# Order of the expert weights' loads around the last writes of x in a three-stage kernel

## The chip, the cores and the metric

The kernel runs on one core of one Trainium2 chip. A core has five engines with queues of their own: PE (TensorE, matmuls into PSUM), DVE (VectorE), ACT (ScalarE), POOL (GpSimd) and SP (SyncE, which here issues the loads and stores). They wait for each other through semaphores. Sixteen DMA engines move data between DRAM and SBUF. The metric is the device time of one execution in microseconds (us).

## What is computed

The reference chains three stages for 2 batches of 768 tokens, all in float32. First a linear attention with 8 heads of 64 and a decaying state. Then a feed-forward block with a gate, 512 to 1024 to 512 columns, whose hidden values pass through a convolution over three tokens. Then a mixture of 8 experts, of which each token uses one:

```
def _attn_ref(q, k, v):
    for t in range(S):
        state = gamma * state + einsum('bhd,bhe->bhde', k[:, :, t], v[:, :, t])
        y[:, :, t] = scale * einsum('bhd,bhde->bhe', q[:, :, t], state)

def _moe_ref(x, w_in, conv_w, w_out):
    h = maximum(x @ w_in, 0)
    conv_out = sum of conv_w[k] * (h moved by k - 1 tokens), k = 0, 1, 2
    return (h * sigmoid(conv_out)) @ w_out

def _moe2_ref(x, w_gate, w_local, w1, w2):
    logits = x @ w_gate;  local = sigmoid(x @ w_local)
    for each token s:  e = argmax(logits[s]) if s == 0 or local[s] < 0.5 else the e before it
        out[s] = softmax(logits[s])[e] * (maximum(x[s] @ w1[e], 0) @ w2[e])
```

## The kernel before, in words

The order of all instructions is written out by hand; the program runs straight on, and nothing reorders it on the chip except that each engine waits for what its next instruction needs.

The second stage's output for one group of 128 tokens is `x_ps` in PSUM (`ffn_out`). ACT copies it to SBUF (`xn`, for the last two groups `xl`, L501), and SP writes it to the DRAM buffer `xs` (L503). Each batch has six groups. In the second batch, four of the six writes are from `xn` and the fifth and sixth from `xl`. The units of this last part are counted by `n`, one for each group and block of 128 hidden columns; the fourth group is complete at `n` = 24, the fifth at 32, the sixth at 40.

The third stage works on tiles of 128 tokens that share an expert. GpSimd gathers a tile's tokens from `xs` by an index table `it` (`gather`, L740 and L741: a memset of the tile `xg`, then an indirect DMA of 256 KB). The first two gathers (tiles 0 and 1, issued at `n` = 27) read only the rows of the first ten writes; the tokens of the last two groups reach tiles 0 and 1 from `xl` in SBUF by four matmuls with one-hot matrices (`late_x`, L836). The third gather is that of the first quarter tile, and it and all later ones read all of `xs`, so they wait for the sixth write.

A tile is turned with matmuls against the identity (L830 for tiles 0 and 1, L817 else), multiplied by w1 (`g1`, PSUM tile `g`), put through a relu by ACT (`hr`, L868), turned again, and multiplied by w2 (`g2`, PSUM tile `y`). There is one PSUM tile `g`, so a tile's first product starts when ACT has read the one before. The result goes out scaled (`yo`, L879) by a scatter of GpSimd (L880). For accuracy each product is three matmuls of a high and a low part (`mm3`, L133 to L135); ACT and DVE make the two parts of the weights (`cut`, L731 and L732) into slots `ws0h`, `ws0l`, `ws1h` and `wc`.

Weights come by SP. `fetch(j, which)` issues four loads of 512 KB of tile j's w1 or w2 into the raw buffer `r` (L710). From tile 2 on a load carries a condition and moves nothing if the tile two before it had the same expert. `fetch_q(g, which, i)` loads four pieces of 512 KB for a quarter tile (L722): tokens of four experts, 32 of each, share one tile. The pieces alternate between two buffers, `qc` and `qs1l`. A group of quarters (`group`) is a generator: one step turns the gathered quarters and ACT copies them to `xq` (L901), the next ones multiply (`hq_ps`, L909, then `yq_ps`, L931). `QT` lists the numbers of the calls of `hook()` at which the next step is emitted; tiles 0 and 1 have the first two calls, and every later tile four.

All of SP's transfers are in one queue in the order of the program. Their landings are told by eight semaphores taken in turn, so SP issues a transfer when the one eight before it has landed.

Of the kernel before, what the change touches and what calls it, by code (L numbers as in the profile page):

```python
# [91 lines left out]
def tile_kernel(ctx, tc, cat, cst, qT, kT, kN, vN, w_in, conv_w, w_out, wg, w1, w2, out):  # L92
# [393 lines left out]
    def ffn_out(b, t, ms):  # L486

        ts = slice(t * P, (t + 1) * P)
        if ms[0] == 0:
            OUT[b, t] = psb.tile([P, DM], F32, tag="x2", name="x2_ps")  # L490
        ps = OUT[b, t]
        for m in ms:
            g = hg[b, m]
            mm3(ps, g[:, 0, ts], g[:, 1, ts], wo_hi[:, m, :], wo_lo[:, m, :], m == 0, m == 7)
        if ms[-1] == 7:
            if b == B - 1 and t >= NG - 2:
                xn = xpool[0].tile([P, DM], F32, name=f"xl{t}", bufs=1)
                LAST.append(xn)
            else:
                xn = rt.tile([P, DM], F32, name="xn", bufs=2)  # L500
            se.activation(out=xn, in_=OUT.pop((b, t)), func=AF.Copy)  # L501
            r = b * S + t * P
            sy.dma_start(out=xs[r:r + P, :], in_=xn)  # L503
# [183 lines left out]
    def home(tag):  # L687
        return big if tag[0] == "s" else ws if tag == "c4" else wx

    def expert_at(n):  # L690
        return sy.value_load(ei[0:1, 0, n:n + 1], min_val=0, max_val=E - 1)

    def raw(lane, which):
        if (lane, which) not in RAW:
            RAW[lane, which] = (wx if lane and which else ws).tile([P, 4, 1024], F32, name=f"r{lane}{which}")
        return RAW[lane, which]

    def fetch(j, which, parts=range(4)):

        src = (w1, w2)[which].rearrange("e p a n -> e p (a n)")  # L700
        kw = {}
        if j == 0:
            src = src[0]
        else:
            src = src[bass.ds(expert_at(j), 1)].rearrange("o p n -> (o p) n")
            if j > 1:
                kw = dict(cond=sy.value_load(ei[0:1, 1, j:j + 1], min_val=0, max_val=1), cond_hint=True)
        dst = raw(j % 2, which)
        for i in parts:
            sy.dma_start(out=dst[:, i, :], in_=src[:, i * 1024:(i + 1) * 1024], **kw)  # L710

    def fetch_q(g, which, i, parts=range(4)):

        if (g, which, i) not in QW:
            tag = QSLOT[nq[0] % 2]
            nq[0] += 1
            QW[g, which, i] = home(tag).tile([P, 4, 1024], F32, tag=tag, name="q" + tag)
        w = QW[g, which, i]
        src = (w1, w2)[which].rearrange("e p a n -> e p (a n)")
        for u in parts:  # L720
            one_e = src[bass.ds(expert_at(NTILE + 4 * g + u), 1)].rearrange("o p n -> (o p) n")
            sy.dma_start(out=w[:, u, :], in_=one_e[:, i * 1024:(i + 1) * 1024])  # L722

    def cut(j, which, i):

        tag = SLOT[ncut[0] % len(SLOT)]
        ncut[0] += 1
        w = home(tag).tile([P, 2, 2, 1024], F32R, tag=tag, name="w" + tag)
        for h in range(2):
            r = RAW[j % 2, which][:, 2 * i + h, :]  # L730
            se.activation(out=w[:, 0, h, :], in_=r, func=AF.Copy)  # L731
            ve.tensor_tensor(out=w[:, 1, h, :], in0=r, in1=w[:, 0, h, :].bitcast(F32), op=ALU.subtract)  # L732
        W[j, which, i] = w.rearrange("p s h n -> p s (h n)")
# [3 lines left out]
    def gather(j, n=NT):  # L737

        X[j] = xg = xpool[0].tile([P, DM], F32, name="xg")
        po.memset(xg, 0.0)  # L740
        return po.indirect_dma_start(out=xg, out_offset=None, in_=xs[0:n], in_offset=bass.IndirectOffsetOnAxis(ap=it[:, j:j + 1], axis=0),  # L741
                                     bounds_check=n - 1, oob_is_err=False)
# [45 lines left out]
    for n, (t, m) in enumerate(units, 1):  # L788
        ffn_out(1, t, (m,))
        for step in STEPS.get(n, ()):  # L790
            next(step, done)
        if n in (18, 24):
            fetch(1, 0, range(2) if n == 18 else range(2, 4))
        if n in (20, 28):
            cut(0, 0, n // 28)
        if n == 27:
            for j in range(2):
                gather(j, NT - 2 * P)
        if n in (27, 32):
            fetch_q(0, 0, 0, range(3) if n == 27 else range(3, 4))  # L800
    p2_stack.close()
    q_stack.close()
    lg_stack.close()
# [133 lines left out]
                yield  # L937


    QT = [3, 8, 8, 9, 13, 18] + [19, 22, 26, 26, 27, 31, 36]  # L940
    groups = []
    hooks = [0]

    def hook():
        hooks[0] += 1
        while QT and QT[0] <= hooks[0]:
            QT.pop(0)
            while groups and next(groups[0], done) is done:
                groups.pop(0)

    def experts(n):

        fetch(1, 1)
        fetch_q(0, 0, 1)
        for j in range(2):
            begin_x(j)
        for j in range(2):
            turn_x(j)
        gather(NTILE)
        gather(2)  # L960
        groups.extend(group(g, g + 1 < QSTAT) for g in range(QSTAT))
        h = tile_g1()
        for i in range(2):
            g1(0, i, h)
            cut(1, 0, i)
            if i:
                relu(0, h)
            hook()
        cut(0, 1, 0)
        fetch(2, 0)  # L970
        T = {}
        for j in range(n):
            last, ahead = j + 1 == n, j + 2 < n
            if j + 3 < n:
                fetch(j + 3, 0)
            if j > 0:
                finish(j - 1)
            if j + 3 < n:
                gather(j + 3)
            if j == 2:  # L980
                gather(NTILE + 1)
            if j not in T and j > 0:
                T[j] = turn_h(j)
            if not last:
                h = tile_g1()
                g1(j + 1, 0, h)
                if j == 0:
                    next(groups[0])
                    T[j] = turn_h(j)
                    cut(0, 1, 1)  # L990
                if ahead:
                    cut(j + 2, 0, 0)
                hook()
                g1(j + 1, 1, h)
                if ahead:
                    cut(j + 2, 0, 1)
                relu(j + 1, h)
                hook()
            if ahead:
                turn_x(j + 2)  # L1000
                fetch(j + 2, 1)
            Y[j] = y = psb.tile([P, 512], F32, tag="b", name="y")
            for i in range(2):
                g2(j, i, T[j], y)
                if not last:
                    cut(j + 1, 1, i)
                    if not ahead and i == 0:
                        T[j + 1] = turn_h(j + 1)
                    hook()
        finish(n - 1)  # L1010
        assert not QT

# [68 lines left out]
```

## Time and profile before

| | us |
|---|---|
| median of 3 runs | 427.65 (425.49 to 429.69) |
| the profiled execution | 422.35 |
| its span, first to last instruction | 420.5 |
| PE busy | 402.5 (96%) |
| DVE busy | 290.1 (69%) |
| ACT busy | 256.3 (61%) |
| POOL busy | 93.7 (22%) |

The page is taken from one execution. Busy times are sums over the span, and a stage can be full on an engine whose share of the whole is low. A row of a timeline has its start, its length, the engine, the line and the tile written and read (out<-in); what the engine waited for stands in brackets. For SP a row is the issue of transfers, not the transfers. In the row of a stretch, the DMA share is the mean busy share of the sixteen DMA engines, and it can come out a little above 1, since a packet counts with its whole length where it starts.

### The profile page before, as it was taken

How to read it: one execution, taken by the hardware profiler on the slowest of the kernel's cores; microseconds unless marked ns; L12 is line 12 of the kernel's file. 1: busy time of each engine (PE TensorE's matmuls, PEld its weight loads, DVE VectorE, ACT ScalarE, POOL GpSimd, SP SyncE). 2: the span in 40 equal slices, each digit the busy share in tenths (PEclk: the TensorE clock that was granted, in tenths of full speed). 3: DMA queues.
4: the chain of work that ended last, by engine and by line, in shares of the span. 5: the costliest groups of instructions: out<-in, count | busy, mean ns of one | idle time of the engine just before them, and what ended most of it. 6: DMA issues, size and time to landing. Idle time of an engine off the chain costs nothing.

```text
span 420.5 us, 7242 instructions
## 1 busy us (share of the span) xinstructions
PE 402.5 (96%) x2412; PEld 328.2 (78%) x2412; DVE 290.1 (69%) x494; ACT 256.3 (61%) x405; POOL 93.7 (22%) x92
## 2 busy tenths in 40 slices
PE   8999999999999999999999789999998999999991
PEld 7898999998987888988778676776766667676881
DVE  3789989798873630578997077959673885958650
ACT  2787778578663323666514178868574786858560
POOL 4356756230200000000001220305304202201210
PEclk9999999999999999999999999999999999999997
DMA  7989872330000101000398999999969999684100
GB/s 238 391 298 397 283 243 60 102 85 16 2 2 0 64 38 50 2 0 2 112 339 311 391 365 345 338 408 409 399 251 367 371 377 388 242 257 197 45 23 33
DMA packets 27324, 86.59 MB, mean 206 GB/s; under 512 B 3598, under 2 KB 4622, under 8 KB 27280
## 3 DMA queue, kind: packets, MB, share of 16 engines
q1 hardware_dynamic: 25200, 79.76, 51.7%
q0 software_dynamic: 2080, 6.29, 3.8%
q8 instruction: 21, 0.34, 0.3%
q14 instruction: 23, 0.19, 0.1%
HBM read 105.18 MB, written 6.55 MB: 266 GB/s over the span
## 4 chain that ended last, share of the span: by engine, by line
PE 47%; issue 25%; DMA 18%; DVE 4%; POOL 2%; ACT 1%; SPq 1%; POOLq 0%
DMA out_dram<-yo,it 16%; PE h_ps L133 6%; PE x_ps L133 6%; PE h_ps L134 5%; PE h_ps L135 5%; PE x_ps L135 5%; PE x_ps L134 5%; PE y L303 3%; PE s_ps L283 3%; PE y L305 2%; PE lg L356 2%; PE wc_ps L194 2%; DMA kq<-in_qT_dram 1%; DMA xs<-xl 1%; POOL xg L741 1%
## 5 line engine op out<-in xcount | busy, mean ns | idle before, releaser
L880 POOL DMA_INDIRECT out_dram<-yo,it x13 | 17.0, 1311 | 133.1 <-ACT yo L879 133.1
L133 PE MATMUL h_ps<-xT,wih 128*128 128x384 f32 x128 | 46.6, 364 | 0.1
L741 POOL DMA_INDIRECT xg<-xs,it x13 | 18.9, 1451 | 121.4 <-DMA r<-in_w_dram 111.1
L365 DVE SCALAR_TENSOR_TENSOR cc<-h,cw,cc 128x768 f32<-128x768 f32 x32 | 34.8, 1088 | 15.8 <-ACT cc L362 15.8
L134 PE MATMUL h_ps<-xT,wih 128*128 128x384 f32 x128 | 43.1, 337 | 0.0
L135 PE MATMUL h_ps<-xT,wil 128*128 128x384 f32 x128 | 43.0, 336 | 0.0
L133 PE MATMUL x_ps<-woh,hg 128*128 128x512 f32 x96 | 38.5, 401 | 0.0
L135 PE MATMUL x_ps<-woh,hg 128*128 128x512 f32 x96 | 37.5, 391 | 0.0
L134 PE MATMUL x_ps<-wol,hg 128*128 128x512 f32 x96 | 37.5, 390 | 0.0
L154 POOL TENSOR_TENSOR na<-na,raw 128x512 int32<-128x512 int32 (+1 forms) x17 | 23.0, 1354 | 50.8 <-DVE na L152 25.8
L732 DVE TENSOR_TENSOR ws0h<-r,ws0h 128x1024 fp32r<-128x1024 f32 x22 | 26.0, 1222 | 8.0 <-ACT ws0h L731 8.0
L732 DVE TENSOR_TENSOR ws1h<-r,ws1h 128x1024 fp32r<-128x1024 f32 x22 | 26.0, 1222 | 8.0 <-ACT ws1h L731 6.0
L732 DVE TENSOR_TENSOR wc<-r,wc 128x1024 fp32r<-128x1024 f32 x22 | 26.0, 1221 | 7.9 <-ACT wc L731 7.9
L303 PE MATMUL y<-at,vz 128*128 128x128 f32 x192 | 29.5, 275 | 0.8 <-ACT vz L278 0.8
L732 DVE TENSOR_TENSOR ws0l<-r,ws0l 128x1024 fp32r<-128x1024 f32 x22 | 26.0, 1221 | 6.2 <-ACT ws0l L731 6.0
L283 PE MATMUL s_ps<-qz,kq 128*128 128x256 f32 x96 | 29.1, 386 | 1.0 <-DVE qz L252 1.0
L731 ACT ACTIVATE wc<-r 128x1024 fp32r<-128x1024 f32 x22 | 22.1, 1055 | 11.2 <-PE g L135 11.2
L731 ACT ACTIVATE ws0l<-r 128x1024 fp32r<-128x1024 f32 x22 | 22.1, 1057 | 9.0 <-PE y L135 9.0
L303 PEld LDWEIGHTS y<-at,vz 128*128 128x128 f32 x192 | 25.9, 192 | 1.4 <-ACT vz L278 1.0
L133 PEld LDWEIGHTS h_ps<-xT,wih 128*128 128x128 f32 x128 | 24.1, 189 | 3.3 <-issue 2.1
L285 DVE TENSOR_TENSOR at<-s_ps,ca 128x256 f32<-128x256 f32 x48 | 20.2, 420 | 8.2 <-PE s_ps L283 7.6
L501 ACT ACTIVATE xn<-x_ps 128x512 f32<-128x512 f32 x10 | 6.0, 597 | 31.1 <-PE x_ps L135 13.8
(234 smaller groups left out, 1036.0 us busy)
## 6 DMA issues: line engine op xcount, KB each, us to landing
r<-in_w_dram SPq DMA_DIRECT2D x88, 512.0 KB
qc<-in_w_dram SPq DMA_DIRECT2D x32, 512.0 KB
qs1l<-in_w_dram SPq DMA_DIRECT2D x32, 512.0 KB
raw<-in_w_in_dram SPq DMA_DIRECT2D x8, 512.0 KB
raw<-in_w_out_dram SPq DMA_DIRECT2D x8, 512.0 KB
kq<-in_qT_dram SPq DMA_DIRECT2D x7, 384.0 KB
kq<-in_kT_dram SPq DMA_DIRECT2D x7, 384.0 KB
kv<-in_vN_dram SPq DMA_DIRECT2D x7, 384.0 KB
```

The source lines that it names most:

```text
L133: te.matmul(ps, lhi, rhi, start=first, stop=False)
L134: te.matmul(ps, lhi, rlo, start=False, stop=False)
L135: te.matmul(ps, llo, rhi, start=False, stop=last)
L154: po.tensor_tensor(out=a, in0=a, in1=lo, op=ALU.add)
L283: te.matmul(ps, self.kq[:, 0, tok], self.qz[:, :, tok], start=True, stop=True)
L285: ve.tensor_tensor(out=self.at[c], in0=ps, in1=self.dm, op=ALU.mult)
L303: te.matmul(y, vz[:, c, j, :], at[:, j, :], start=(j == 0), stop=(c == 0 and j == 1))
L365: ve.scalar_tensor_tensor(out=cc, in0=h[:, i:i + S], scalar=cw[:, m, i:i + 1], in1=cc, op0=ALU.mult, op1=ALU.add)
L731: se.activation(out=w[:, 0, h, :], in_=r, func=AF.Copy)
L732: ve.tensor_tensor(out=w[:, 1, h, :], in0=r, in1=w[:, 0, h, :].bitcast(F32), op=ALU.subtract)
L741: return po.indirect_dma_start(out=xg, out_offset=None, in_=xs[0:n], in_offset=bass.IndirectOffsetOnAxis(ap=it[:, j:j + 1], axis=0), bound ...
L880: po.indirect_dma_start(out=out, out_offset=bass.IndirectOffsetOnAxis(ap=it[:, j:j + 1], axis=0), in_=yo, in_offset=None, bounds_check=NT ...
```

## The change

Three things move, and nothing is added or left out. The loads of tile 1's w1, before in two halves at `n` = 18 and 24, and the first four quarter pieces, before at 27 and 32, are issued behind the fifth write (`n` = 32), except two of the pieces, which come behind the sixth (`n` = 40). The quarters' second piece is issued ahead of tile 1's w2 instead of behind it. And the step that turns the quarters is emitted earlier for the first group (hook 2 instead of inside tile 0's turn) and later for the second group (hook 20 instead of 19).

```
@@ -789,15 +789,15 @@
-        if n in (18, 24):
-            fetch(1, 0, range(2) if n == 18 else range(2, 4))
...
-        if n in (27, 32):
-            fetch_q(0, 0, 0, range(3) if n == 27 else range(3, 4))
+        if n == 32:
+            fetch(1, 0)
+        if n in (32, 40):
+            fetch_q(0, 0, 0, range(2) if n == 32 else range(2, 4))
...
-    QT = [3, 8, 8, 9, 13, 18] + [19, 22, 26, 26, 27, 31, 36]
+    QT = [2, 3, 8, 8, 9, 13, 18] + [20, 22, 26, 26, 27, 31, 36]
...
     def experts(n):
 
+        fetch_q(0, 0, 1)
         fetch(1, 1)
-        fetch_q(0, 0, 1)
...
                 if j == 0:
-                    next(groups[0])
                     T[j] = turn_h(j)
```

SP's queue before, from the second batch's third write of `xn` on. `r_2037` takes tile 1's w1, `qc_2338` the first quarter piece; the rows left out are the reading of the expert's number and what else comes with each issue.

```order
L503 DMA xs<-xn 128x512 x3
...
L710 DMA r_2037<-in_w_dram 128x1024
...
L503 DMA xs<-xn 128x512
...
L710 DMA r_2037<-in_w_dram 128x1024
...
L722 DMA qc_2338<-in_w_dram 128x1024
...
L503 DMA xs<-xl_2389 128x512
...
L722 DMA qc_2338<-in_w_dram 128x1024
L503 DMA xs<-xl_2427 128x512
...
L710 DMA r_2460<-in_w_dram 128x1024
...
L722 DMA qs1l<-in_w_dram 128x1024
```

The same place of the changed kernel; `r_2492` takes tile 1's w2.

```order
L503 DMA xs<-xn 128x512 x4
L503 DMA xs<-xl_2336 128x512
...
L710 DMA r_2037<-in_w_dram 128x1024
...
L722 DMA qc_2352<-in_w_dram 128x1024
...
L503 DMA xs<-xl_2398 128x512
...
L722 DMA qc_2352<-in_w_dram 128x1024
...
L722 DMA qs1l<-in_w_dram 128x1024
...
L710 DMA r_2492<-in_w_dram 128x1024
```

Before, two loads of `r_2037` stand on each side of the fourth write, three pieces ahead of the fifth write and one ahead of the sixth. Now the fourth and fifth writes follow each other, and four loads and two pieces stand between the fifth and the sixth; the other two pieces and the four of `qs1l` are ahead of w2.

PE between tile 0's first product (`g_2550`) and the quarters' product, before:

```order
L135 MATMUL g_2550<-ws0l,xl 128x512
L133 MATMUL g_2642<-ws1h,xh 128x512
...
L135 MATMUL g_2642<-ws1h,xl 128x512
L817 MATMUL tp<-cs,xg 128x128 x4
L817 MATMUL tp<-cs,hr 128x128 x8
L909 MATMUL hq_ps<-qc_2338,xq 32x512 x8
```

And of the changed kernel:

```order
L135 MATMUL g_2541<-ws0l,xl 128x512
L817 MATMUL tp<-cs,xg 128x128 x4
L133 MATMUL g_2640<-ws1h,xh 128x512
...
L135 MATMUL g_2640<-ws1h,xl 128x512
L817 MATMUL tp<-cs,hr 128x128 x8
L909 MATMUL hq_ps<-qc_2352,xq 32x512 x8
```

The four transposes of the gathered quarters (`tp<-cs,xg`) moved from behind the first half of tile 1's first product (12 matmuls) to ahead of it.

ACT at the same place, where the copy of those transposes (`xq`) passes the cut of w2 of tile 0 into `ws0h`; before:

```order
L868 ACTIVATE hr<-g_2550 128x512 x2
L731 ACTIVATE ws0h<-r_2032 128x1024 x2
L901 ACTIVATE xq<-tp 128x512
L821 ACTIVATE th<-tp 128x512 x2
L731 ACTIVATE ws0l<-r_2032 128x1024 x2
```

And of the changed kernel:

```order
L868 ACTIVATE hr<-g_2541 128x512 x2
L901 ACTIVATE xq<-tp 128x512
L731 ACTIVATE ws0h<-r_2032 128x1024 x2
L821 ACTIVATE th<-tp 128x512 x2
L731 ACTIVATE ws0l<-r_2032 128x1024 x2
```

The copy moved one cut up; everything else of ACT is in the same order here.

## Rows read from the trace of the kernel before

**Rows 1.** The page, part 1: engine, busy us (share of the span) and instructions.
```profile
PE 402.5 (96%) x2412; PEld 328.2 (78%) x2412; DVE 290.1 (69%) x494; ACT 256.3 (61%) x405; POOL 93.7 (22%) x92
```

**Rows 2.** Stretches: us, busy us (count) by engine, granted clock, DMA share, GB/s.
```profile
224.00:232.00 8.00, 8.00 (x38) 6.66 (x38) 4.49 (x11) 1.16 (x2) 2.76 (x3) 1.00 1.00 383
248.00:274.00 26.00, 25.56 (x152) 17.69 (x156) 20.93 (x21) 20.97 (x28) 3.75 (x3) 1.00 0.94 341
274.00:310.00 36.00, 36.00 (x199) 27.07 (x192) 25.99 (x26) 26.48 (x36) 9.87 (x8) 1.00 1.02 404
```

**Rows 3.** PE's timeline, 233 to 253 us: start, us, line, instructions [idle before <- releaser].
```profile
235.78 1.13 PE L830 MATMUL tp<-cs,xg 128*128 128x128 f32 x8 [2.22 <-DMA xg<-xs,it]
...
248.44 0.50 PE L133 MATMUL g<-ws1h,xh 128*128 128x512 f32 x1 [1.18 <-ACT hr L868]
...
251.30 0.60 PE L817 MATMUL tp<-cs,xg 128*128 128x128 f32 x4
251.74 1.04 PE L817 MATMUL tp<-cs,hr 128*128 128x128 f32 x8
```

**Rows 4.** SP's timeline, DMA issues: start, us from first to last of a row.
```profile
205.72 3.73 SPq L710 DMA_DIRECT2D r<-in_w_dram  x8
...
221.74 0.91 SPq L710 DMA_DIRECT2D r<-in_w_dram  x2
222.75 0.37 SPq L503 DMA_DIRECT2D xs<-xn  x1
223.92 0.88 SPq L710 DMA_DIRECT2D r<-in_w_dram  x2
225.59 2.61 SPq L722 DMA_DIRECT2D qc<-in_w_dram  x3
228.75 0.33 SPq L503 DMA_DIRECT2D xs<-xl  x1
```

**Rows 5.** GpSimd's timeline, the gathers' starts.
```profile
228.96 1.21 POOL L741 DMA_INDIRECT xg<-xs,it  x1 [111.14 <-DMA r<-in_w_dram]
...
231.00 1.01 POOL L741 DMA_INDIRECT xg<-xs,it  x1 [0.28 <-POOL xg L740]
...
239.77 1.00 POOL L741 DMA_INDIRECT xg<-xs,it  x1 [7.23 <-DMA xs<-xl]
```

**Rows 6.** The chain of waits, 234 us: start, us, what.
```profile
234.22 4.78 DMA xs<-xl
```

**Rows 7.** Tile xg, 225 to 420 us: time from a gather's start to its landing.
```profile
DMA to landing us min/median/max: 4.2/7.0/7.9
```

**Rows 8.** DMA, 205 to 212 us in 40 slices of 0.175 us: rate.
```profile
GB/s 0 0 0 0 0 0 0 0 0 94 70 94 187 234 304 328 257 398 445 398 398 398 468 421 398 374 421 328 398 304 375 445 421 374 375 351 375 468 351 445
```

**Rows 9.** ACT's timeline, two cuts of weights.
```profile
248.28 2.01 ACT L731 ACTIVATE ws0h<-r 128x1024 fp32r<-128x1024 f32 x2
...
262.67 2.01 ACT L731 ACTIVATE ws0h<-r 128x1024 fp32r<-128x1024 f32 x2
```

**Rows 10.** PE's timeline, the gap at 321 us.
```profile
321.84 0.66 PE L817 MATMUL tp<-cs,xg 128*128 128x128 f32 x4 [0.85 <-ACT yo L879]
```

**Rows 11.** SP's timeline and wait at 311.8 us, and PE's timeline behind it.
```profile
311.82 0.07 SPq L710 DMA_DIRECT2D r<-in_w_dram  x1
SPq L710 <- DMA qs1l<-in_w_dram: 0.9, 1, 0.9
312.11 1.90 PE L931 MATMUL yq_ps<-qs1l,tq 128*32 128x512 f32 x16
```

**Rows 12.** Stretches around PE's last matmul, columns as in rows 2.
```profile
410.00:412.00 2.00, 1.92 (x9) 1.26 (x7) 0.00 (x0) 0.00 (x0) 0.00 (x0) 1.00 0.07 25
415.00:416.00 1.00, 0.00 (x0) 0.00 (x0) 0.00 (x0) 0.00 (x0) 0.00 (x0) 0.79 0.69 266
```

**Rows 13.** PE's timeline at the program's start.
```profile
1.07 4.21 PE L212 MATMUL lg<-st 128*128 128x128 f32 x18 [1.07 <-DVE st L204]
...
5.92 1.99 PE L212 MATMUL lg<-st 128*128 128x128 f32 x16
```

## The prediction

> **What bounds the kernel now.** I read the page first. PE is busy for 402.5 of the 420.5 us [rows 1], so the end of the program is the end of PE's work, and only PE's gaps and what opens new ones matter. Next I took the share by stretches: in 274 to 310 us PE is busy for all 36.00 us, while the DMA engines run at a share of 1.02 and 404 GB/s [rows 2]. Two things are full at once there, PE and the loads. Then I read PE's timeline where the change acts, 233 to 252 us. It has two gaps: the first matmuls on a gathered tile (`xg`) start at 235.78 after 2.22 us, and tile 1's first product at 248.44 after 1.18 us, for ACT's `hr`, which empties the PSUM tile of tile 0's first product. The quarters' four transposes take 251.30 to 251.74 [rows 3].
>
> The first wait goes back to SP's queue. The fourth write of `x` in this half is issued at 222.75, with two loads of 512 KB 1 us ahead of it and two more 1.2 us behind [rows 4]. GpSimd's first gather, which reads all that the first ten writes wrote, starts only at 228.96 [rows 5].
>
> **The change part by part.** Three terms make the sum.
>
> *Term 1, the write is freed.* In 222.75 to 228.75 SP now issues nothing but that write. What a write takes alone no row shows. The sixth, behind loads, took 4.78 us [rows 6], so this one lands by 227.5. Gathers start 0.77 us after a write lands (239.00 to 239.77 [rows 5, 6]), here by 228.3, and take 4.2 to 7.9 us, median 7.0 [rows 7]. The worst sum is 236.2, no better than before; the best is about 230. The engines are quiet until 232, which speaks for the 4.2, so the tile is there by 232.5 and PE goes on at 233.56: **2.22 us earlier** (bounds 0 to 2.22). The second gather follows 2.04 us later and is wanted two groups of matmuls later (1.9 us), so it holds nothing up. The sixth write's data come from ACT at 234.20, before PE wants them. Everything up to the end of tile 0's first product moves by these 2.22 us.
>
> *Term 2, the quarters' transposes.* They now stand ahead of tile 1's first product, in the hole that waits for `hr`. Were their gathered tile there, the product would start at 248.44 - 2.22 = 246.22, and the transposes behind it would come 2.22 + 0.44 = 2.66 us earlier than before. That is all that this change can give. But this tile is the third gather, and it waits for the sixth write. SP now issues, behind the fifth write (228.75), four loads and two quarter pieces ahead of the sixth. By the spacings of SP's rows (1.17 us from a write to a load, 0.91 for two loads, 2.61 for three pieces) they fit in before 234.2, so the write is issued as early as before, but behind six loads of 0.524 MB. From an idle queue to the full rate takes about 2.4 us (issue 205.72, full rate in the 18th slot of 0.175 us [rows 4, 8]). The loads thus flow from 228.75 + 1.17 + 2.4 = 232.3; 3.15 MB at 404 GB/s is 7.8 us, the write's own 0.26 MB 0.65 us. It lands at 240.7, or up to 1 us later for what no row splits off; I take 241.0, against 239.00 before. Then 0.77 us to the gather's start and 7.0 us to its landing, as the engines are full then: 248.8. The transposes take 0.44 us, and tile 1's first product starts at 249.25. Before, without the transposes that stood behind it, it would be level at 248.44 + 0.44 = 248.88. So terms 1 and 2 together **cost 0.4 us**. Bounds: with the fastest gather (4.2 us) it starts at 246.4, a gain of 2.4; with the slowest (7.9) and the write at 242 a loss of 2.3.
>
> A bandwidth of the Trainium skill can be set beside this term. "DMA: Bandwidth & Descriptors", section "Specifications", gives a fabric ceiling of 435 GB/s and an HBM limit of about 358 GB/s for one core. The 404 GB/s of [rows 2] lies above that limit, so the trace does not agree with it. By the ceiling, as an estimate from that page, the write would land 0.6 us earlier and terms 1 and 2 come out at -0.2 us; by the limit 1.1 us later and at +1.5.
>
> ACT's copy `xq` behind the transposes moves ahead of the cut of `ws0h` (2.01 us from 248.28 [rows 9]). That cut and all behind it on ACT now wait until about 249.8, 1.5 us; its result is used by tile 0's second product, which PE reaches only behind the quarters' 32 matmuls and the second half of tile 1's first product, so this is hidden. The quarters' second piece goes ahead of tile 1's w2 on SP. Between 240.7 and w2's landing stand 10 loads and three gathers, 6.0 MB, 14.9 us at 404 GB/s: 255.6, some us more where gathers share the engines. ACT first cuts it at 262.67 [rows 9], so 7 us cover that. The second quarters' transposes go from ahead of half of a product to behind it, still ahead of the transposes that wait 0.85 us at 321.84 for ACT's `yo` [rows 10]. Work moved between two points ahead of a wait leaves its end where it is: 0.
>
> *Term 3, loads are late.* In 224 to 232 us the engines moved 383 x 8 = 3.06 MB [rows 2]. Now they have in those 8 us the fourth and fifth writes and two gathers, 4 x 0.26 = 1.05 MB. The missing 2.0 MB are 5.0 us at 404 GB/s, and all later loads stand behind them on one queue. They can catch up only where the engines had room. In 248 to 274 us they ran at 341 GB/s: measured against 404, room for 63 x 26 = 1.64 MB or 4.1 us; by their share, 0.94 against 1.02, 2.1 us. The lower holds if SP's issuing and its waits for buffers made the gaps and go on making them. I take the middle, 3.1: the lag is 1.9 us at 274 (bounds 0.9 to 2.9), and stays, as 274 to 310 has none to spare. The load with the least cover on the way is the last `qs1l` piece of the first quarters: SP waits for its landing to use the semaphore again and goes on at 311.82, and PE takes the piece at 312.11 [rows 11], 0.3 us later. So at 312.11 PE is 1.9 - 0.3 = **1.6 us late** against before. The 0.4 us of terms 1 and 2 is inside this, since a PE that is late already waits less. From there SP's next loads wait for PE to free the buffers, and all shift together.
>
> Sum: 0.4 + 1.2 = 1.6 us on the profiled execution's own 422.35 us (span 420.5 and 1.85 around it), 423.95. The median of the runs, 427.65, lies 5.3 above that execution; I add the 1.6 to the median: 429.3 us.
>
> **Rivals.** *A, it comes in time.* The third gather lands in 4.2 us and the loads catch up within 0.3 us: the full 2.66 us are gained, 425.0 us. For it: 2.22 us of wait do go, and the room by rates is 4.1 of 5.0 us. Against it: the gather then shares the engines with the loads that were held back, and of thirteen only the fastest took 4.2 us [rows 7]. Chance 0.18. *B, the lag stays (slower side).* Nothing is caught up: PE waits at 312.11 for 5.0 - 0.3 = 4.7 us, 432.35 us. It decides above 1% once less than 0.5 of the 5.0 us is recovered. For it: the room in 248 to 274 may be SP's and not the engines'. Chance 0.13. *C, the clock falls.* PE now sits idle from about 245 to 248.8, 3.9 us. After PE's last matmul, which ended at 411.9, the granted clock was still 1.00 at 415 and 0.79 in the us after, so it fell some 3.7 us into idleness [rows 12]; the gaps of 2.22 and 1.18 us left it at 1.00 in 248 to 274 [rows 2]. At the start 18 small matmuls took 4.21 us (0.23 each) and from 5.92 on 16 took 1.99 (0.12 each) [rows 13]: some 4.8 us at the lower level, 1.2 GHz, of which half, 2.4 us, is loss. Here that makes 0.4 + 2.4 = 2.8 us, 430.45 us. Chance 0.12. The Trainium skill, "TensorE: Matmul & The Clock Gate", Part 1, states this rule: the array falls to half its clock when idle and must be kept busy to regain it. By that rule the new wait is a risk that the old gaps were not; the end of this trace agrees. *D, nothing changes.* The first gather is held by something that the late write hid, such as its index table, so the 2.22 us stay; the rest of the hole takes the transposes, and the lag is recovered: about 427.65 us. Nothing in the rows speaks for it but that they do not show the table's end. Chance 0.07.
>
> **How the numbers follow.** The forecast has 0.50, A 0.18, B 0.13, C 0.12, D 0.07. 429.3 is the forecast's. The range 425.0 to 432.0 holds A, C, D and most of the forecast's own bounds, and leaves out B and the ends. About 1% (4.3 us) is what a measurement of this kernel can tell from no change, as its own runs lie 4.2 us apart. Faster by that needs more than the 2.66 us there are: 0.03. Slower by it is B with a little of C: 0.14. Within it: 0.83.
>
> **What would show it.** Term 1: the first gather starts near 226 to 228 and PE's wait at 235.78 is gone. Term 2: PE waits up to 4 us for `xg` ahead of tile 1's first product, which starts at about 249.2, and the sixth write takes about 6.8 instead of 4.78 us. Term 3: the engines are nearly empty in 225 to 232, SP's waits for `qs1l` pieces end about 2 us later, and PE has a new wait of about 1.2 us ahead of the matmuls that stood at 312.11. I am wrong if the third gather lands before 246, if no wait shows at 312, if PE waits for a piece before that, or if the granted clock drops in 245 to 252.

## The result: slower by 0.8%, inside the range

The changed kernel takes 429.87 us (median of 22 runs, 427.68 to 432.61); the kernel before, run beside it, 426.65 (22 runs). The ratio is 1.0083, with a 95% interval of 1.0058 to 1.0108: 3.5 us slower. The forecast was 429.3 us in a range of 425.0 to 432.0 and "within 1%" as likeliest; it held. But the forecast's step was +1.6 us and the measured one is +3.5, so a term was mis-sized. The interval, 2.5 to 4.6 us, holds rival C's 2.8 and just misses B's 4.7, so the size alone does not choose between them. The profiled execution of the changed kernel took 429.40 us (span 427.5); that of the kernel before, at 422.35, lies well below its own median.

The page of the changed kernel, part 1 (columns as in [rows 1]):

```profile
PE 406.3 (95%) x2412; PEld 330.9 (77%) x2412; DVE 290.0 (68%) x494; ACT 256.5 (60%) x405; POOL 93.8 (22%) x92
```

PE is busy for 3.8 us more than in [rows 1] with the same instructions, and its share falls. The stretches of [rows 2], now, with two more (231 to 240 and 232 to 248 us):

```profile
224.00:232.00 8.00, 8.00 (x40) 6.71 (x40) 4.78 (x12) 1.42 (x2) 3.63 (x4) 1.00 0.42 126
231.00:240.00 9.00, 9.00 (x64) 8.09 (x63) 0.80 (x2) 1.93 (x4) 0.00 (x0) 1.00 0.96 320
232.00:248.00 16.00, 13.03 (x81) 11.04 (x79) 6.02 (x6) 6.67 (x9) 2.87 (x3) 1.00 1.00 370
248.00:274.00 26.00, 22.27 (x116) 16.38 (x117) 15.92 (x15) 16.04 (x21) 2.16 (x4) 0.87 1.00 372
274.00:310.00 36.00, 36.00 (x208) 25.47 (x207) 26.22 (x28) 25.78 (x34) 12.64 (x11) 1.00 1.01 383
```

And 232 to 248 us of the kernel before, which the rows ahead of the prediction do not have:

```profile
232.00:248.00 16.00, 13.05 (x79) 10.78 (x77) 6.02 (x6) 6.28 (x9) 5.42 (x7) 1.00 1.02 390
```

In 224 to 232 us the engines now move a third of what they moved, as forecast. In 248 to 274 us, where loads were to catch up, PE is idle for 3.7 of 26 us (0.4 before) and the granted clock is 0.87.

PE's timeline of the changed kernel, 233 to 258 us (columns as in [rows 3]):

```profile
233.71 1.05 PE L830 MATMUL tp<-cs,xg 128*128 128x128 f32 x8
...
239.02 0.50 PE L133 MATMUL g<-ws0h,xh 128*128 128x512 f32 x1
...
251.73 1.11 PE L817 MATMUL tp<-cs,xg 128*128 128x128 f32 x4 [6.69 <-DMA xg<-xs,it]
252.49 0.78 PE L133 MATMUL g<-ws1h,xh 128*128 128x512 f32 x1
...
257.14 1.03 PE L817 MATMUL tp<-cs,hr 128*128 128x128 f32 x8
```

The wait at 235.78 of [rows 3] is gone. In its place PE waits 6.69 us for the third gather, and the 12 matmuls from 252.49 to 257.14 take 4.65 us, where they took 2.86 before. The cause of the second number stands in the granted clock of three stretches:

```profile
244.00:249.00 5.00, 1.03 (x5) 0.53 (x3) 1.48 (x2) 1.08 (x2) 3.60 (x5) 1.00 1.03 415
250.00:256.00 6.00, 4.27 (x12) 3.56 (x13) 1.55 (x2) 2.49 (x3) 0.00 (x0) 0.50 1.00 389
257.00:262.00 5.00, 5.00 (x43) 2.08 (x42) 3.45 (x4) 4.22 (x6) 0.00 (x0) 1.00 0.97 342
```

Within the wait the clock fell from 2.4 GHz (1.00) to 1.2 GHz (0.50), and it was back at 2.4 GHz by 257. SP's issues, GpSimd's gathers and the sixth write in the chain of waits (as [rows 4 to 6]):

```profile
222.96 0.32 SPq L503 DMA_DIRECT2D xs<-xn  x1
229.05 0.32 SPq L503 DMA_DIRECT2D xs<-xl  x1
230.46 1.95 SPq L710 DMA_DIRECT2D r<-in_w_dram  x4
233.22 1.47 SPq L722 DMA_DIRECT2D qc<-in_w_dram  x2
234.80 0.57 SPq L503 DMA_DIRECT2D xs<-xl  x1
```

```profile
226.36 1.21 POOL L741 DMA_INDIRECT xg<-xs,it  x1 [108.25 <-DVE pr L677]
...
244.86 1.50 POOL L741 DMA_INDIRECT xg<-xs,it  x1 [14.58 <-DMA qc<-in_w_dram]
```

```profile
234.80 9.32 DMA xs<-xl
```

The fourth write stands alone, the first gather starts at 226.36, but the sixth write takes 9.32 us and the third gather starts at 244.86. Last, the place of [rows 10, 11]: the product that uses the last `qs1l` piece, 5.45 us later than before and now 2.53 us long instead of 1.90, and the gap behind it, 6.71 us later.

```profile
317.56 2.53 PE L931 MATMUL yq_ps<-qs1l,tq 128*32 128x512 f32 x16
...
328.55 0.66 PE L817 MATMUL tp<-cs,xg 128*128 128x128 f32 x4 [1.52 <-ACT yo L879]
```

### The profile page after: what moved, and what is told of

Same layout as the page of the kernel before. It is cut to its first block, busy times and chain, and to the rows that moved or that the text cites. A ratio compares the mean times of both kernels' runs of the same rounds, so it can differ in the third digit from the quotient of the medians.

```text
span 427.5 us, 7239 instructions
## 1 busy us (share of the span) xinstructions
PE 406.3 (95%) x2412; PEld 330.9 (77%) x2412; DVE 290.0 (68%) x494; ACT 256.5 (60%) x405; POOL 93.8 (22%) x92
## 4 chain that ended last, share of the span: by engine, by line
PE 41%; issue 25%; DMA 19%; DVE 6%; ACT 3%; SPq 2%; POOL 2%; POOLq 0%
DMA out_dram<-yo,it 16%; PE x_ps L133 5%; PE x_ps L135 5%; PE x_ps L134 5%; PE h_ps L133 4%; PE h_ps L134 4%; PE h_ps L135 4%; PE y L303 3%; PE s_ps L283 3%; DMA xs<-xl 2%; PE y L305 2%; DVE cc L365 2%; PE wc_ps L194 2%; DMA kq<-in_qT_dram 1%; PE lg L356 1%
## 5 line engine op out<-in xcount | busy, mean ns | idle before, releaser
L741 POOL DMA_INDIRECT xg<-xs,it x13 | 18.9, 1454 | 125.8 <-DVE pr L677 108.3
```

## The experiments

Each was timed beside the kernel before (426.5 to 427.1 us there), on the same chip as it; three chips were used, so versions of different groups are compared by their ratios. A ratio is not the quotient of the two medians and differs from it by up to 0.4%; its interval says what can be told. "Last product" below is the quarters' `yq_ps<-qs1l`, which needs the last piece of the first group and which ended at 314.01 in [rows 11]. A trace is one execution, and executions stand up to 2.5 us apart already where PE gets to the first turned tile (`tp`, L830), ahead of the place where the change can make PE wait; the table behind the experiments therefore also counts from there.

**The kernel before once more.** No edit; it gives the size of a difference that means nothing.

> The kernel before once more, unchanged, for the size of the differences that mean nothing: a ratio of 1.000 within 0.3%. Its trace is a second execution to set beside the first, which was 4.3 us below the median. By the theory that the kernel before itself has executions with a longer wait for the first gather, a fall of the granted clock behind it and a fall at about 328, this one shows some of these where it lies nearer the median.

426.98 us, ratio 0.998 (0.9944 to 1.0016). Its trace (425.09 us) lies nearer to the median:

```profile
236.90 1.13 PE L830 MATMUL tp<-cs,xg 128*128 128x128 f32 x8 [3.04 <-DMA xg<-xs,it]
...
313.13 2.72 PE L931 MATMUL yq_ps<-qs1l,tq 128*32 128x512 f32 x16
```

The first gather is waited for 3.04 us instead of 2.22, and the last product ends at 315.85 instead of 314.01. So the profiled execution on which the prediction rests is a good one of its kind, by some 2 us at this place.

**The transposes alone.** The kernel before with only the last two hunks of the change:

```
-    QT = [3, 8, 8, 9, 13, 18] + [19, 22, 26, 26, 27, 31, 36]
+    QT = [2, 3, 8, 8, 9, 13, 18] + [20, 22, 26, 26, 27, 31, 36]
-                    next(groups[0])
```

> Of the change only the quarters' transposes move (earlier for the first group, one hook later for the second); all loads and writes stand as in the kernel before. Late gather (the sixth write behind the loads is what costs): the sixth write and so the third gather come as before (landing near 246.8 us), PE reaches the transposes at 247.1 and does not wait, the hole of 1.18 us takes their 0.44 us: about -0.4 us, ratio 0.999. Late loads (the lag of all loads is what costs): no load moves, so 0 us, ratio 1.000; even a gain of 0.4 us would be given back at the last qs1l piece of the first quarters, which PE takes 0.3 us after it lands. Clock: no long wait, the clock stays at 1.00, 0 us.

427.45 us, ratio 0.9994 (0.9962 to 1.0027): no difference that can be told, and at most 1.2 us of the 3.5. Its one trace (428.70 us) shows what an execution can do with no load moved: PE waits 3.90 us for the first gather, the granted clock falls to 0.50, and the last product ends at 317.89, 3.9 us later than in the first execution of the kernel before.

**The loads alone.** All of the change but those two hunks.

> Of the change only the loads move; the quarters' transposes stand as in the kernel before, behind the first half of tile 1's first product. Late gather: PE reaches the transposes at about 249.1 us, the third gather lands near 251.7 as in the changed kernel, so PE waits 2.6 us instead of 6.7, the clock does not fall, and the kernel is +0.4 to +1 us against before (ratio 1.001 to 1.002). Late loads: the loads are as late as in the changed kernel, whose last piece of the first quarters landed 6.4 us later than before; PE, which is hardly late by then, waits 4 to 5 us for it near 312 us, and the kernel comes out as slow as the changed one, +3.5 to +5 us (ratio 1.008 to 1.012). Clock: without the long wait only what the loads cost is left; between the two.

430.25 us, ratio 1.0046 (1.0012 to 1.0080): slower. By the medians the whole loss is here (3.5 us), by the ratio 2.0 us of it. PE's timeline at the two places:

```profile
251.54 0.66 PE L817 MATMUL tp<-cs,xg 128*128 128x128 f32 x4 [2.71 <-DMA xg<-xs,it]
...
313.03 1.05 PE L931 MATMUL yq_ps<-qs1l,tq 128*32 128x512 f32 x2
314.31 1.05 PE L931 MATMUL yq_ps<-qs1l,tq 128*32 128x512 f32 x2 [0.23 <-DMA qs1l<-in_w_dram]
...
316.82 1.90 PE L931 MATMUL yq_ps<-qs1l,tq 128*32 128x512 f32 x10 [0.20 <-DMA qs1l<-in_w_dram]
```

Behind the first half of tile 1's product PE waits 2.71 us for the gather, and the clock stays up there (1.00 in 249 to 262). So the loss does not need the fall of the clock in the changed kernel. Then, at 313, it takes the last product's matmuls two by two as the pieces land: 5.69 us instead of 1.90.

**The clock kept up.** The changed kernel with 24 matmuls of the identity, whose result nothing uses, in the wait for the gather:

```
+                scr = psq.tile([P, 2, 512], F32, tag="q", name="warm")
+                for _ in range(24):
+                    te.matmul(scr[:, 0, 0:P], ident, ident, start=True, stop=True)
```

> The changed kernel with 24 matmuls of 128 x 128 of the identity into a free PSUM tile ahead of the quarters' transposes (about 6 us of PE work into the wait of 6.7 us; their result is not used). Clock (the fall of the clock is what costs): the granted clock stays at 1.00 in 245 to 260 us, tile 1's product takes 2.9 instead of 4.7 us, and the kernel gains 2.1 us on the changed one, +1.4 us against before (ratio 1.003). Late loads: PE is 2.1 us earlier at 257 but waits that much longer for the last quarter piece near 317 us, so the time is that of the changed kernel (ratio 1.008). Late gather: the gain of 2.1 us stays, as for the clock.

429.15 us, ratio 1.0048 (1.0014 to 1.0083), beside 429.87 and 1.0083 for the change: 0.7 us less by the medians, 1.5 by the ratios, whose intervals overlap. The clock was held, and PE waited at the last product nevertheless (the second fence starts where PE reaches the first turned tile, at 233.71 in the changed kernel):

```profile
244.00:249.00 5.00, 5.00 (x34) 4.53 (x33) 3.29 (x3) 2.54 (x4) 2.13 (x3) 1.00 1.03 419
249.00:262.00 13.00, 11.59 (x88) 7.96 (x88) 5.97 (x7) 6.97 (x9) 2.52 (x3) 1.00 1.00 380
```

```profile
235.51 1.05 PE L830 MATMUL tp<-cs,xg 128*128 128x128 f32 x8
...
317.29 2.73 PE L931 MATMUL yq_ps<-qs1l,tq 128*32 128x512 f32 x16
```

Matmuls that need 1.90 us took 2.73 from 317.29 on, and ended at 320.02, where the changed kernel's ended at 320.09. But this execution was 1.80 us later from the start: counted from the first turned tile, PE reached the last product 2.07 us earlier than in the changed kernel, waited there 0.2 us more, and ended it 1.87 us earlier. Then the clock fell once more, behind 328, which cost this execution some 1.6 us. So what the fall of the clock at 250 cost is not settled: neither nothing nor the 2.1 us that the theory of the clock had promised is excluded, and two executions of the kernel before differ by 1.5 us in the same count. The Trainium skill, "TensorE: Matmul & The Clock Gate", Part 1, has the clock follow how busy the array is kept; the stretch at 1.00, with the matmuls put in, agrees.

**The loads one write earlier.** The kernel before with all four w1 loads behind the fourth write:

```
-        if n in (18, 24):
-            fetch(1, 0, range(2) if n == 18 else range(2, 4))
+        if n == 24:
+            fetch(1, 0)
```

> The kernel before with all four loads of tile 1's w1 behind the fourth write of x (the first two stood ahead of it); all else as before. Late gather: the fourth write lands near 225 us, the first gather starts near 226.4, the wait of 2.22 us is gone and nothing else moves: -2.2 us, ratio 0.995. Late loads: two loads start 2 us later, the queue loses about 1 us, and PE, now 2.2 us earlier, only waits 2.2 us and that 1 us longer for the last quarter piece near 312 us: 0 to +1 us, ratio 1.000 to 1.002, with a new PE wait of 2 to 3 us there.

425.41 us, ratio 0.9978 (0.9942 to 1.0014): not slower, and between what the two theories had promised (0.995 for the gather, 1.000 to 1.002 for the loads). It is 4.8 us below the loads alone by the medians and 2.9 by the ratios, both measured beside the same runs. Here the fourth write is free as in the change; the first load is issued at 224.51. The two versions differ in more than the place of these four loads: here the quarter pieces and the order of the second piece and w2 are as before.

```profile
223.08 0.32 SPq L503 DMA_DIRECT2D xs<-xn  x1
224.51 1.95 SPq L710 DMA_DIRECT2D r<-in_w_dram  x4
```

**All loads behind the sixth write.** The changed kernel with

```
-        if n == 32:
+        if n == 40:
             fetch(1, 0)
-        if n in (32, 40):
-            fetch_q(0, 0, 0, range(2) if n == 32 else range(2, 4))
+            fetch_q(0, 0, 0)
```

> The changed kernel with all six loads (the second tile's w1 and the quarters' first) behind the sixth write of x instead of four behind the fifth and two behind the sixth. The sixth write is then alone on the queue, so the third gather, which follows it, starts about 5 us earlier. Late gather: the wait of 6.7 us for it is gone and with it the fall of the clock behind it, and the time falls by 4 us or more, to about 425. Late loads: the four loads start about 4 us later still, nothing is recovered up to the quarters' last piece, whose product waits 6 to 8 us more than in the kernel before, and the time rises by about 2 to 4 us to some 432 to 434. Were both true, the gain at 250 and the loss at 317 cancel, and it stays at 430.

434.61 us (6 runs), ratio 1.0172 (1.0116 to 1.0228). The third gather starts at 238.60 and nothing waits for it any more, yet this is the slowest. SP's timeline, ACT's at 245 us and PE's (this kernel is one line shorter, so L867 is L868 elsewhere and L930 is L931):

```profile
230.35 5.80 SPq L503 DMA_DIRECT2D xs<-xl  x2
237.25 2.02 SPq L710 DMA_DIRECT2D r<-in_w_dram  x4
```

```profile
246.94 1.06 ACT L731 ACTIVATE wc<-r 128x1024 fp32r<-128x1024 f32 x1 [1.22 <-DMA r<-in_w_dram]
248.76 1.06 ACT L731 ACTIVATE wc<-r 128x1024 fp32r<-128x1024 f32 x1 [0.76 <-DMA r<-in_w_dram]
249.72 1.07 ACT L867 ACTIVATE hr<-g 128x512 f32<-128x512 f32 x2
```

```profile
250.84 0.80 PE L133 MATMUL g<-ws1h,xh 128*128 128x512 f32 x1 [4.07 <-ACT hr L867]
...
319.41 2.18 PE L930 MATMUL yq_ps<-qs1l,tq 128*32 128x512 f32 x6
321.79 1.90 PE L930 MATMUL yq_ps<-qs1l,tq 128*32 128x512 f32 x10 [0.20 <-DMA qs1l<-in_w_dram]
```

The two w1 cuts at 246.94 and 248.76 wait for loads. ACT takes its work in order, so `hr`, which stands behind them, comes at 249.72, and PE waits 4.07 us: the name in the bracket is ACT's, the cause is a load. The granted clock falls at the end of that wait too (0.51 in 250 to 256). At 319.41 the last product waits again. So late loads cost PE at two places here, and not all of the 4.7 us above the change (3.8 by the ratios) need be the queue's.

**The gather in time, the loads late.** The loads alone, as above, but the quarters' first two pieces too behind the sixth write, so that four loads instead of six stand ahead of it:

```
-        if n in (32, 40):
-            fetch_q(0, 0, 0, range(2) if n == 32 else range(2, 4))
+        if n == 40:
+            fetch_q(0, 0, 0)
```

> The changed kernel's loads with the transposes as before, but the first two loads of the quarters behind the sixth write of x too, so that only the four of w1 stand ahead of that write. It should land at about 241 instead of 244 and the third gather at about 248, 3 us earlier, while all loads from there on end when they did. Late gather: the wait of 2.71 us for it is gone and the time falls by about 3 us, from 430.25 to 427. Late loads: the tensor engine comes earlier by the same 3 us to the product of the quarters' last w1 piece and stands there for 6 to 7 us instead of 3.8, and the time stays at about 430.

429.25 us, ratio 1.0066 (1.0029 to 1.0104), beside 1.0046 without this edit: unchanged.

```profile
248.74 0.66 PE L817 MATMUL tp<-cs,xg 128*128 128x128 f32 x4 [0.27 <-DMA xg<-xs,it]
...
316.49 1.90 PE L931 MATMUL yq_ps<-qs1l,tq 128*32 128x512 f32 x10 [0.20 <-DMA qs1l<-in_w_dram]
```

The wait for the gather fell from 2.71 to 0.27 us, and the last product still ended only at 318.39 (318.72 without the edit); counted from the first turned tile both end after 85.4 us. The time won at 249 was waited away before 318: 1.4 us for pieces at 273 to 275, the rest at the last product, which took 4.32 us from 314.07 on.

**Slack at the last product.** The quarters' last product and the whole second group one hook later:

```
-    QT = [3, 8, 8, 9, 13, 18] + [19, 22, 26, 26, 27, 31, 36]
+    QT = [3, 8, 8, 9, 13, 19] + [20, 23, 27, 27, 28, 32, 37]
```

It was put into the kernel before, into the loads alone, into the version with both (gather in time, and slack), and into the version with the loads behind the fourth write.

> The kernel before, with the last product of the first group of quarters and everything of the second group put one hook later, so that the product that needs the last piece of the quarters' w1 comes about 3 us after that piece has landed instead of 0.3 us. If the queue of loads binds the kernel before up to 312 us (its last piece landed at 311.70, its product started at 312.11), whatever the tensor engine gains ahead of that place is given back there, and so slack there frees it: executions in which the piece comes late lose that wait of 0 to 2 us, so the median falls by 0 to 1.5 us. If only the gathers at 234 to 250 set the time, nothing changes (within 0.5 us). If the later quarters' results come late for the end instead, the time rises by 1 to 2 us, to be seen as a wait for the second group's results at the end.

425.97 us, ratio 0.9987 (0.9942 to 1.0033): no difference that can be told.

> The changed kernel's loads with the transposes as before, and the quarters' last product and second group one hook later. In the trace of that version alone the tensor engine stood 3.8 us in the product of the last w1 piece (5.69 us instead of 1.90). Late loads: the slack of about 3 us removes most of that, and the time falls by 2.5 to 3.5 us from 430.25, to about 427. Late gather: the wait for the third gather (2.71 us at 251.5 in that version) stays and nothing is won, 430. A mixture, with the gather's share left over, would be 428 to 429.

430.11 us, ratio 1.0082 (1.0046 to 1.0118): nothing won, against what the theory of late loads had promised in that place.

> The same with the quarters' last product and second group one hook later: third gather 3 us earlier and about 3 us of slack at the last w1 piece. In the version with that slack alone (430.11) the wait at the last piece was gone, but the wait for the third gather (2.69 us) and the slower clock behind it were left, and 1.2 us of wait at the second group's first w1 piece at 338. If the two costs overlap, so that each has to go before the other shows, this version falls by about 3 us, to 427. If only the loads' lag counts, down to the second group, it gives back all at 338 and stays at 430. If only the late gather counts, it falls to 427 like the version without the slack.

430.61 us, ratio 1.0069 (1.0034 to 1.0105): nothing won either. In the version with the slack alone the last product takes its 1.90 us from 319.41 on and waits for nothing, but PE waits elsewhere; its waits in 220 to 345 us (in all, times, longest), with the slack alone and then with both:

```profile
PE tp L817 <- DMA xg<-xs,it: 2.7, 1, 2.7
PE hq_ps L909 <- DMA qs1l<-in_w_dram: 1.5, 3, 1.0
...
```

```profile
PE hq_ps L909 <- DMA qs1l<-in_w_dram: 3.2, 6, 0.9
...
PE tp L817 <- DMA xg<-xs,it: 0.3, 1, 0.3
```

With the gather in time the wait for `xg` falls from 2.7 to 0.3 us, and the waits for `qs1l` pieces grow from 1.5 to 3.2. Three of these stand at 254 to 277, three at 338 to 342, in the second group's first product, some 20 us behind the place that was given slack:

```profile
338.52 1.04 PE L909 MATMUL hq_ps<-qs1l,xq 128*32 128x512 f32 x2 [0.23 <-DMA qs1l<-in_w_dram]
340.49 1.05 PE L909 MATMUL hq_ps<-qs1l,xq 128*32 128x512 f32 x2 [0.93 <-DMA qs1l<-in_w_dram]
342.40 1.06 PE L909 MATMUL hq_ps<-qs1l,xq 128*32 128x512 f32 x8 [0.86 <-DMA qs1l<-in_w_dram]
```

So slack at one consumer does not take the wait for pieces away; PE waits at others. The waits at 338 to 342 are in part the slack's own: the kernel before with the same slack waits 0.9 us for a piece at 337, and in this version the engines are at shares of 0.68 to 0.73 in 315 to 325 us, with the second group's pieces issued only from 324.49 on (314.95 in the kernel before, once more). That they are the first group's lag handed on is not shown.

> The version with all four w1 loads behind the fourth write of x, and with the quarters' last product and second group one hook later. In that version's trace alone the product of the quarters' last w1 piece took 3.18 us instead of 1.90 (piece landed at 312.65), so by the theory of late loads the slack takes away those 1.3 us and the smaller ones of other executions: 1 to 1.5 us below that version's 425.41, so about 424, 2.5 us below the kernel before. If that product's wait costs nothing (the following waits for tile results absorb it), it stays at 425.4. By the theory of late gathers, 425.4 as well, since the first gather already starts at 226.3.

424.50 us, ratio 0.9949 (0.9911 to 0.9988): faster than the kernel before, by 0.1 to 0.9%, and than the changed one. PE's waits in 220 to 345 us are these three:

```profile
PE g L133 <- ACT hr L868: 1.2, 1, 1.2
PE hq_ps L909 <- DMA qs1l<-in_w_dram: 1.1, 1, 1.1
PE tp L830 <- DMA xg<-xs,it: 0.4, 1, 0.4
```

Whether the slack adds to the loads behind the fourth write (0.9978 alone) can't be told: the intervals overlap.

**All runs side by side.** By the issue of the first w1 load in the trace, and the median time: 221.74 us, 426.65 (before); 222.54, 426.98 (before, once more); 221.59, 427.45 (transposes alone); 224.51, 425.41 (behind the fourth write); 229.74, 429.25 (gather in time); 230.06, 430.25 (loads alone); 230.46, 429.87 (the change); 232.27, 429.15 (clock kept up); 237.25, 434.61 (behind the sixth). With the slack: 223.96, 425.97 (before); 224.51, 424.50; 231.74, 430.11; 231.35, 430.61. Up to 224.5 nothing is lost; 5 to 8 us later the time is 4 to 6 us longer, 13 us later 9. The issue times hold what an execution was early or late by before, up to 2.5 us.

In the next table, "first tile" is the time at which PE is ready for the first turned tile (the start of its matmuls less the wait for the gather), and "last product" the end of that product. The versions with slack are left out, since there the product stands at another place.

| kernel | first tile, us | last product, us | between them, us | execution, us | behind the last product, us |
|---|---|---|---|---|---|
| before, first execution | 233.56 | 314.01 | 80.5 | 422.35 | 108.3 |
| behind the fourth write | 233.47 | 314.59 | 81.1 | 423.80 | 109.2 |
| before, once more | 233.86 | 315.85 | 82.0 | 425.09 | 109.2 |
| gather in time | 232.98 | 318.39 | 85.4 | 427.88 | 109.5 |
| the change | 233.71 | 320.09 | 86.4 | 429.40 | 109.3 |
| behind the sixth write | 235.01 | 323.69 | 88.7 | 433.37 | 109.7 |
| transposes alone | 233.22 | 317.89 | 84.7 | 428.70 | 110.8 |
| loads alone | 233.34 | 318.72 | 85.4 | 429.97 | 111.3 |
| clock kept up | 235.51 | 320.02 | 84.5 | 431.01 | 111.0 |

In the last three the granted clock fell once more, behind the gap at 326 to 328 us (0.79 in 326 to 334), which is the extra 1.6 us. Apart from that the time varies by 1.4 us once this product has ended, and in all but the first row PE waits in it for the piece. Between the first tile and this product the versions with late loads need 84.5 to 88.7 us, the kernel before 80.5 and 82.0; the transposes alone, with 84.7, show that one execution can lose as much on PE's side.

## Why the prediction held, and which step failed

*What bounds the kernel* was right: in 274 to 310 us PE and the loads are both full. The versions with late loads show more: there PE comes to the last product and waits for the load, so of the two it is the loads that hold.

*Term 1, the write is freed: right.* The first gather was to start at 226 to 228 and started at 226.36; PE was to go on at 233.56 and did at 233.71; tile 0's first product, forecast at 241.26 - 2.22 = 239.04, started at 239.02. The 2.22 us were won, at that place.

*Term 2, the quarters' transposes: mis-sized, beyond its own bounds.* The sixth write was to take 6.8 us and took 9.32, landing at 244.12 instead of 241.0. In 231 to 240 us the engines moved 320 GB/s, not the 404 of [rows 2]: the 2.4 us to the full rate, read from eight loads issued into an idle queue [rows 8], did not hold for this start. With four loads ahead of it instead of six (the gather in time) the write took 6.83 us. The gather was then issued 0.74 us after the write landed (0.77 forecast) and landed in 6.8 (7.0): both right. Tile 1's first product started at 252.49 instead of 249.25.

*Rival C, the clock: it happened, at the size it was given.* One of the prediction's signs of being wrong came true: the granted clock dropped within 245 to 252 us, to 0.50 from 249.6 on. From start to start, the first half of tile 1's product took 4.65 us instead of 2.86 and the transposes 0.76 instead of 0.44: 2.1 us, where 2.4 was forecast. (The prediction read 4.8 us at 1.2 GHz from the slow matmuls of [rows 13]; the granted clock from 0 to 6 us is 1.00 in the trace, so what the rows show is half the pace, and not the lower clock. In the changed kernel 6.8 us ran at 0.50.) The transposes of `hr`, at 251.74 in [rows 3], came at 257.14: terms 1 and 2 with the clock cost 5.4 us there, not 0.4. How much of the 2.1 us stayed in the time is open, by the version with the clock kept up. It is not the whole price: the loads alone, the gather in time and the version with both lose 2.0 to 2.9 us by their ratios with the clock at 1.00 in 249 to 262.

*Term 3, loads are late: the size was right, the recovery failed.* This is the step that was mis-sized. The bytes that the changed kernel moved less than the first execution of the kernel before, from the stretches above and [rows 2], and their time at 404 GB/s:

| stretch, us | before, GB/s | changed, GB/s | missing, MB | us |
|---|---|---|---|---|
| 224 to 232 | 383 | 126 | 2.06 | 5.1 |
| 232 to 248 | 390 | 370 | 0.32 | 0.8 |
| 248 to 274 | 341 | 372 | -0.81 | -2.0 |
| 274 to 310 | 404 | 383 | 0.76 | 1.9 |
| in all | | | 2.33 | 5.8 |

The first row is what was forecast (2.0 MB). The second the prediction left out. In the third the loads caught up 2.0 us, just below the bounds of 2.1 to 4.1 and not the 3.1 taken, so the lag at 274 was 3.9 us and not 1.9. In the fourth, said to have nothing to spare and nothing to lose, they fell back again. So 5.8 us were missing at 310, and the last product ended 6.1 us later. Against the second execution of the kernel before (361, 407, 325 and 399 GB/s in the four stretches) the same count gives 1.83 MB, 4.5 us, and the product 4.2 us later.

The count tells how far the loads are behind and not why: with the transposes alone 1.53 MB were missing too, but nearly all of it lost in 248 to 274 at a share of 0.80, behind a PE that was late, where with late loads the share is 0.99 to 1.01. Part of the drop in 274 to 310 is scatter: the versions whose loads are not late ran at 394 to 406 GB/s there, those with late loads at 371 to 399. The share of the engines was 1.01, so the queue was not idle; what made a byte dearer no run here isolates. So the lag went the way of **rival B**: in the end nothing was recovered.

*The wait at the last product: there, but smaller.* PE was to come nearly in time and to wait about 1.2 us. In the changed kernel it came 5.45 us late by itself and waited 0.63, so this trace alone does not tell whether PE or the loads held the end. The loads alone and the gather in time do: with the loads as late PE came at 313.03 and 314.07, and the product ended only at 318.72 and 318.39.

*The sum.* 1.6 us were added to the median, and 3.5 came out. The time itself was met to 0.6 us, partly by chance: the median of the runs beside the change lay 1.0 us below the one shown. And it is 3.5, not the 6.1 us by which the last product is later, since the first execution of the kernel before was a good one: the product ended at 315.85 in its second, and at 317.89 with the transposes alone. That the gather's delay lies inside the loads' lag and does not add to it was right: the gather in time shows it. The other two experiments do not: with the clock kept up part of the time may have been won, and all loads behind the sixth write moves the loads further and brings a wait of its own.

*What was costed at nothing.* The transposes moved: nothing that can be told, as forecast (0.9994). The second piece ahead of w2 was not tried apart from the loads, and every version with late loads has it; the two together are the 3.5 us of the version with the loads alone (430.25 against 426.71). No wait of PE for that w2 shows in the traces of the change and of the loads alone, but that the order costs nothing is not shown.

*What stays open.* How the 3.5 us divide between the late loads, the order of the second piece and w2, and the clock; why the rate in 274 to 310 us is lower when the loads are late; and why slack of one hook gives nothing to the kernel before. That the queue is full from 231 to 310 us (shares of 0.96 to 1.01 in the changed kernel's stretches) is why a late start is not made up there; it was not measured by a version with fewer bytes.

## What to carry to other kernels

Where the loads run at the engines' full rate for a long stretch, look at when the first byte enters it: holding loads back to free a small write can cost that delay at the far end, and what is won at the write is then waited away on the way there. Free the write by putting the loads right behind it, not behind the next ones; tile 1's loads one write earlier, with the rest as before, cost nothing that can be told (0.9978). Two traces are compared from a point ahead of the change, not from their starts: here that point alone moved by up to 2.5 us. Before a wait is priced, follow the path on to the next place that the load queue binds, since a wait ahead of that place may be worth nothing.

## What was not expected of the hardware

- The first transfers after a quiet stretch ran below the later rate: 320 GB/s in 231 to 240 us (349 with the loads alone), 404 in 274 to 310 of the kernel before, at shares of 0.96 (0.96) and 1.02.
- The sixth write, 0.26 MB, landed 2.00 us after its issue with no load ahead of it (all loads behind the sixth write), 4.78 in the kernel before, 6.83 behind four loads (gather in time) and 9.32 behind six (the change).
- The granted clock fell in or at the end of waits of 6.69, 4.07, 3.90 and in one case 2.69 us, and stayed up through waits of 3.04, 2.82, 2.71 and 2.22 us. Behind the gap of [rows 10] it fell after waits of 1.54, 1.49 and 1.27 us in three executions and stayed up after 1.41, 1.52, 1.56, 1.62 and 1.66 in five: waits of one length went both ways.
- A wait of 4.07 us for ACT's `hr` was a wait for loads, those of the two cuts that stand ahead of it on ACT.
